# Block sums on Pool with their splits one step later, and the order of ACT's copies in the pair steps

## The chip, the cores and the metric

The kernel runs on one core of a Trainium2 chip. The metric is the device time of one execution in microseconds; the kernel before takes 726.09 us, the median of three runs (724.1 to 730.0).

## The reference

Three layers follow each other. Linear attention without softmax, with an RMS norm per head; a mixture of eight experts with one expert per token; and a two-layer network with an ELU, of width 2048. What comes out of the last is the result.

```python
kv = einsum('bhsd,bhse->bhde', k, v); out = einsum('bhsd,bhde->bhse', q, kv)
x = out / sqrt(mean(out * out) + 1e-6) * g_norm            # 2304 tokens x 512
e = argmax(x @ w_gate); p = softmax(x @ w_gate)[e]
y = p * (relu(x @ w1[e]) @ w2[e])                           # 8 experts, width 1024
h = y @ w_in; g = where(h > 0, h, exp(min(h, 0)) - 1)       # width 2048
return g @ w_out
```

## The kernel before, in words

Every product is made in full precision out of three fast ones: a value is split into a high word (a copy on ACT, `split_hi`, L521) and a low word (value minus high word, `split_lo`, L524, on DVE or Pool), and `three` multiplies high by high, low by high and high by low into one PSUM bank.

**Expert steps.** After the attention, the tokens lie sorted by expert. There are 64 steps `u` (8 experts by 8 pieces of their width), 37 and later in the part that matters here. `step(u)` issues the loads of unit u + 3 (`expert_load`, two DMAs on SP, into the six buffers of the tag "a", which prepared weights `f` share), the first product of unit u (`expert_h`: 12 matmuls into `ph`, then ACT's `hh` and DVE's `hl`), the second product of unit u − 1 (`expert_y`: 12 matmuls into four banks `acc`), and the split of unit u + 2's weights (`expert_split`: `w1h` and `w2h` on ACT, `w1l` and `w2l` on DVE). Some steps also split the next expert's tokens (`window`), or do a stage of preparing the weights of the third layer (`next(parts)`).

**Block sums.** The third layer multiplies `y` (in `yT`) by a Strassen-like scheme for most of its width: seven products of sums of blocks instead of eight. The seven right sides are y blocks and sums of y blocks; they are made once, split, and kept in `y_dram`. `y_block_into` splits a block of 384 tokens (ACT and Pool, four pieces) and stores it. `right_sums` makes the sums: a subtraction on DVE (L895), the split into `th` on ACT and `tl` on DVE, and two DMAs on SP (L885). One call of `next` finishes the sum before (low word and DMAs) and makes one sum with its high word. `early_sums` are 16 such sums, called at the end of the steps in `SUMS` (37, 38, 40, 44, 45, 46, 48, 52, 53, 54, 56, 60 to 64), the last one in the first steps of the next stage; `th` and `tl` have one buffer each (tag "e" has two). `late_sums` are eight, called in steps 1 to 9 of the next stage, with buffers in the unused half of `part`.

**Second block, first quarter.** 24 `ffn_step`s (six blocks by four pieces): first product `ffn_h` (12 matmuls), ACT's two exponential passes, DVE's `g`, then one step later its split (`ffn_g`), and two steps later the second product (`ffn_out`, 9 matmuls), whose accumulators ACT copies to `part` after the fourth piece. In the second step of a block `y_block_into` splits the next one.

**Pair steps.** The other three quarters of the width: `pair_step(w, s)`, 9 times two steps, each with seven products of six matmuls (`product`, L1064) named P1, P5, P2, P6, P3, P7, P4. P1, P6, P7 and P4 add up in one bank `pa`, and between them ACT copies the bank's present sum (`s1`, `u2`, `u3`); PE must wait for that copy before it adds the next product. DVE adds the other banks to the copies; that gives the four results g11, g12, g22 and the one from P4 (here g21). Each goes through `elu` (two ACT passes and one on DVE) and `elu_split`. In `gap(0)` to `gap(3)` stand second-layer products of earlier steps (`unit`, six matmuls and a DVE addition to `part`), and stages of preparing later weights (`next(parts2)`, with splits `ab` of weight sums).

**What sets the order.** All of this up to pair step w = 5 is under `manual_schedule`: each engine runs its instructions in the order in which the code issues them. The pair steps from w = 6 on and the last units are ordered by the framework's planner. Each engine is in order, and so is each queue: on SP a DMA that waits holds back all behind it.

Of the kernel before, what the change touches and what calls it, by code (L numbers as in the profile page):

```python
# [9 lines left out]
F32 = mybir.dt.float32  # L10
F32R = mybir.dt.float32r
# [4 lines left out]
ALU = mybir.AluOpType  # L16
# [25 lines left out]
def block_kernel(ctx, tc, qT, k, v, g_norm, w_gate, w1, w2, w_in, w_out, out, cap, **_):  # L42
# [477 lines left out]
    def split_hi(dst, src):  # L520
        return nc.scalar.activation(dst[0], src, AF.Copy)  # L521

    def split_lo(dst, src, engine):
        return engine.tensor_tensor(out=dst[1], in0=src, in1=dst[0].bitcast(F32), op=ALU.subtract)  # L524
# [50 lines left out]
    def expert_load(u):  # L575
        if u >= NU:
            return
        r, fc = divmod(u, NF)
        if fc == 0:
            load_regs(r)  # L580
        a1 = wst.tile([P, C], F32, name="a1", tag="a", bufs=AB)
        a2 = wst.tile([P, C], F32, name="a2", tag="a", bufs=AB)
        first = nc.sync.dma_start(out=a1, in_=w1[bass.ds(eids[r], 1), fc].rearrange("o p c -> (o p) c"))
        mark["sp"] = nc.sync.dma_start(out=a2, in_=w2[bass.ds(eids[r], 1), fc].rearrange("o p c -> (o p) c"))
        wstage[u] = (a1, a2)
        return first
# [286 lines left out]
            for h, t in enumerate((yh, yl)):  # L873
                nc.sync.dma_start(out=y_dram[n // 2, o][:, h], in_=t[:, k:k + KH].bitcast(F32))

    def right_sums(pieces, tiles):


        last = []

        def finish():
            m, o, k, r, t = last.pop()
            split_lo(t, r, nc.vector)
            for h in range(2):
                nc.sync.dma_start(out=y_dram[m, o][:, h, k], in_=t[h].bitcast(F32))  # L885

        for m, k in pieces:
            b = [[yT[:, h * KH + k, (2 * m + n) * BT:(2 * m + n + 1) * BT] for n in range(2)] for h in range(2)]
            r = None
            for o, x, y in ((5, b[1][1], b[0][1]), (3, b[0][1], b[0][0]), (4, b[1][1], None), (6, b[1][0], None)):  # L890
                if last:
                    finish()
                y = r if y is None else y
                r, t = tiles()
                nc.vector.tensor_tensor(out=r, in0=x, in1=y, op=ALU.subtract)  # L895
                split_hi(t, r)
                last.append((m, o, k, r, t))
                yield
        finish()
        yield  # L900

    def small_tiles():
        t = [hp.tile([P, BT], F32R, name=n, tag="e", bufs=2) for n in ("th", "tl")]
        return hp.tile([P, BT], F32, name="tr", tag="g", bufs=2), t


    assert 3 * (N // E) >= 2 * BT and 6 * (N // E) >= 4 * BT
    early_sums = right_sums([(m, k) for m in range(2) for k in range(KH)], small_tiles)
    SUMS = [u for u in range(4 * NF + 5, NU) if u % NF in (0, 4, 5, 6)]
    SUMS = SUMS[:8] + [u for u in SUMS[8:] if u > 6 * NF] + [NU - 1, NU]  # L910

    APART = 4 * NF + 4
    FIRST = NF + 1
# [3 lines left out]
    def step(u):  # L917
        r, fc = divmod(u, NF)
        if u == 4:
            nc.gpsimd.memset(xT[:, :, N:NS], 0.0)  # L920
        more = r + 1 < E and placed["t"] < need[r + 1]
        expert_load(u + 3)
        if u == FIRST - 1:
            prep_load(2)
        if u < NU:
            expert_h(u)
        q = QUOTA[u] if u < NF else 2 if more else 0
        if q:
            place(min(need[r + 1], placed["t"] + 1), 0)
        if u:  # L930
            expert_y(u - 1)
        if q > 1:
            place(min(need[r + 1], placed["t"] + q - 1), 0)
        if fc == 5 and r + 1 < E:
            place(need[r + 1], 0)
        place_ahead(2)
        expert_split(u + 2, nc.gpsimd if u < NF else nc.vector)
        if fc in (5, 6) and r + 1 < E:
            m = NP // 2
            window(r + 1, (fc - 5) * m, (fc - 4) * m)  # L940
        if FIRST <= u < NU and fc in (1, 2, 3, 7) and done["n"] < 6 * NC2:
            next(parts)
            done["n"] += 1
        if u == APART:
            place(NT, 0)
            beyond_windows()
        if u in SUMS:
            next(early_sums, None)
        if u == NU - 2 and cap >= BT:
            y_block_into(0)  # L950

# [79 lines left out]


    spare = part[:, NT // 2:].rearrange("p i c -> p (i c)")
    turn = {"n": 0}

    def spare_tiles():
        n = turn["n"] = 1 - turn["n"]
        at = [spare[:, (3 * n + i) * BT:(3 * n + i + 1) * BT] for i in range(3)]
        return at[0], (at[1].bitcast(F32R), at[2].bitcast(F32R))

    late_sums = right_sums([(NB // 2 - 1, k) for k in range(KH)], spare_tiles)
    NM = NB // 2
    steps = [(n, c) for n in range(NB) for c in range(NC2)]

# [72 lines left out]
    QUOTAS = ((6, 4), (6, 4), (6, 6))  # L1117
    pend = {}

    def finish_last():  # L1120
        if pend:
            elu_split(*pend.pop("x"))

    def pair_step(w, s):
        between = {n: [] for n in range(3)}
        if s == 0 and w:
            v = w - 1
            between[0] = [lambda: unit(v, 1, 0, 0), lambda: unit(v, 1, 0, 1)]
            between[1] = [lambda: unit(v, 0, 0, 1), lambda: unit(v, 0, 1, 1)]
            between[2] = [lambda: unit(v, 0, 2, 1), lambda: unit(v, 1, 1, 0), lambda: unit(v, 1, 1, 1)]  # L1130
        elif s == 0:
            between[0] = [lambda: ffn_out(*steps[-2], tiles=(0, 1))]
            between[1] = [lambda: ffn_out(*steps[-2], tiles=(2,))]
            between[2] = [lambda: ffn_out(*steps[-1], tiles=(0,))]
        else:
            v = w - 1
            if w:
                between[0] = [lambda: unit(v, 1, 2, 0), lambda: unit(v, 1, 2, 1)]
            else:
                between[0] = [lambda: ffn_out(*steps[-1], tiles=(1, 2))]  # L1140
            between[1] = [lambda: unit(w, 0, 0, 0)]
            between[2] = [lambda: unit(w, 0, 1, 0)]
            if w < NW - 1:
                between[2].append(lambda: unit(w, 0, 2, 0))
        quota = QUOTAS[w % NM][s]

        def gap(n):
            for _ in range(quota * (n + 1) // 4 - quota * n // 4):
                next(parts2, None)
            for f in between.get(n, []):  # L1150
                f()

        A, V = nc.scalar, nc.vector
        pa = ps_h.tile([P, C], F32, name="pa", tag="ph")
        pd = ps_x.tile([P, C], F32, name="pd", tag="pt")
        product(w, s, "P1", pa, True)
        s1 = wt.tile([P, BT], F32, name="s1")
        A.activation(s1, pa[:, :BT], AF.Copy)
        product(w, s, "P5", pd, True)
        s5 = wt.tile([P, BT], F32, name="s5", bufs=1)  # L1160
        A.activation(s5, pd[:, :BT], AF.Copy)
        pe = ps_x.tile([P, C], F32, name="pe", tag="pt")
        product(w, s, "P2", pe, True)
        finish_last()
        V.tensor_tensor(out=s1, in0=s1, in1=pe[:, :BT], op=ALU.add)
        g11 = elu(s1)
        gap(0)
        product(w, s, "P6", pa, False)
        u2 = hp.tile([P, BT], F32, name="u", tag="g", bufs=2)
        A.activation(u2, pa[:, :BT], AF.Copy)  # L1170
        elu_split(w, s, 0, 0, g11)
        product(w, s, "P3", pd, False)
        V.tensor_tensor(out=u2, in0=u2, in1=pd[:, :BT], op=ALU.add)
        g12 = elu(u2)
        gap(1)
        product(w, s, "P7", pa, False)
        u3 = hp.tile([P, BT], F32, name="u", tag="g", bufs=2)
        A.activation(u3, pa[:, :BT], AF.Copy)  # L1178
        elu_split(w, s, 1, 0, g12)
        V.tensor_tensor(out=s5, in0=s5, in1=u3, op=ALU.add)  # L1180
        g22 = elu(s5)
        gap(2)
        product(w, s, "P4", pa, False)
        elu_split(w, s, 1, 1, g22)
        pend["x"] = (w, s, 0, 1, elu(pa[:, :BT]))
        gap(3)

    def ffn_step(s):
        if 1 <= s <= len(steps):
            ffn_g(*steps[s - 1])  # L1190
        if s < len(steps):
            n, c = steps[s]
            ffn_h(n, c)
            if c == 1 and n + 1 < NB:
                y_block_into(n + 1)
        if 2 <= s < len(steps):
            ffn_out(*steps[s - 2])
        if s:
            next(early_sums, None)
            next(late_sums, None)  # L1200
            next(parts2)
        if s >= len(steps) - 4:
            for o in ((0, 3), (1, 4), (2, 5), (6,))[s - len(steps) + 4]:
                right_load(0, o)
# [9 lines left out]
    for w in range(by_hand, NW):  # L1214
        for s in range(2):
            pair_step(w, s)
    finish_last()

    w = NW - 1
    for b, t, ss in ((0, 2, (0,)), (1, 0, (0, 1)), (0, 0, (1,)), (0, 1, (1,)), (0, 2, (1,)), (1, 1, (0, 1)), (1, 2, (0, 1))):  # L1220
# [33 lines left out]
```

## Time and profile before

| | |
|---|---|
| median of three runs | 726.09 us |
| profiled execution | 724.72 us, span 722.9 us |
| PE busy, PEld busy | 683.1 us (94%), 628.6 us (87%) |
| DVE, ACT, POOL busy | 497.6 us (69%), 390.1 us (54%), 105.0 us (15%) |
| mean granted TensorE clock | 0.99 |
| data moved by DMA | 145.89 MB, mean 202 GB/s |

PE is the matmul, PEld the load of its weights, which runs beside the matmul before. Consecutive matmuls overlap in the records, so a busy PE need not be at its best; a PEld that is busy throughout is. The profile names an idle time by what released it ("<-"). Times of instructions contain the start and the end, which overlap with the neighbours: two DVE operations of 0.55 us can follow each other in 0.47 us.

### The profile page before, as it was taken

The page shows a single profiled execution, that of the slowest core. Times are in us where ns is not written, and L with a number is a line of the kernel's source. Part 1 is how long each engine was busy: PE and PEld are TensorE (multiplying, and loading weights), DVE is VectorE, ACT ScalarE, POOL GpSimd, SP SyncE. Part 2 cuts the span into 40 slices and gives each one's busy share as a digit, 9 for nine tenths or more (in the row PEclk, how much of TensorE's full clock was granted, in tenths as well). Part 3 has the DMA queues.
Part 4 walks back from the last instruction along what each step waited for, and adds up shares of the span by engine and source line. Part 5 has one row for each costly group of instructions (what it writes and reads, how often), then busy time and mean ns, then how long its engine had stood idle before and what let it go on. Part 6 is the DMA issues. An engine that isn't in the chain of part 4 may idle for free.

```text
span 722.9 us, 11978 instructions
## 1 busy us (share of the span) xinstructions
PE 683.1 (94%) x4236; PEld 628.6 (87%) x4236; DVE 497.6 (69%) x952; ACT 390.1 (54%) x818; POOL 105.0 (15%) x116
## 2 busy tenths in 40 slices
PE   8988999999989898969999998999999999999996
PEld 7888899999989887958789887988789898998895
DVE  4488768677776687747776646777687778955542
ACT  1463565555554564635665656664666555754550
POOL 7123851000000000022222200000000000002113
PEclk9998999999999999999999999999999999999999
DMA  8996956654555666744543627393637548165512
GB/s 281 395 310 166 295 175 197 185 176 147 187 164 177 216 199 220 218 175 149 197 173 116 260 119 290 134 342 120 264 113 311 230 163 321 59 261 219 205 57 88
DMA packets 67108, 145.89 MB, mean 202 GB/s; under 512 B 9312, under 2 KB 29280, under 8 KB 67040
## 3 DMA queue, kind: packets, MB, share of 16 engines
q1 hardware_dynamic: 63424, 135.44, 54.3%
q0 software_dynamic: 2880, 9.59, 3.8%
q8 instruction: 36, 0.59, 0.3%
q14 instruction: 32, 0.26, 0.1%
q10 hardware_dynamic: 736, 0.02, 0.1%
HBM read 118.92 MB, written 26.10 MB: 201 GB/s over the span
## 4 chain that ended last, share of the span: by engine, by line
PE 32%; issue 12%; DVE 10%; ACT 7%; DMA 3%; POOL 3%; SPq 0%; POOLq 0%; ACTq 0%; DVEq 0%
PE pa L1064 5%; PE acc L1105 3%; PE acc L1106 3%; PE acc L1104 3%; DMA y_dram<-th 3%; PE pd L1064 3%; PE ph L638 2%; PE ph L640 2%; POOL out L1112 2%; PE ph L639 2%; PE acc L1024 2%; PE acc L1025 2%; PE acc L1026 2%; PE pe L1064 1%; ACT e L1081 1%
## 5 line engine op out<-in xcount | busy, mean ns | idle before, releaser
L1064 PE MATMUL pa<-right,ab 128*128 128x384 f32 x432 | 86.1, 339 | 3.5 <-ACT u L1178 1.7
L1064 PEld LDWEIGHTS pa<-right,ab 128*128 128x128 f32 x432 | 76.7, 188 | 10.6 <-ACT u L1178 3.0
L638 PE MATMUL acc<-hh,w2h 128*128 128x288 f32 (+6 forms) x256 | 78.4, 306 | 7.7 <-ACT hh L657 7.7
L638 PE MATMUL ph<-xh,w1h 128*128 128x288 f32 (+6 forms) x256 | 78.2, 305 | 3.4 <-PEq L829 2.4
L640 PE MATMUL acc<-hl,w2h 128*128 128x288 f32 (+6 forms) x256 | 78.0, 305 | 0.0
L640 PE MATMUL ph<-xl,w1h 128*128 128x288 f32 (+6 forms) x256 | 77.7, 303 | 0.3 <-DVE xl L619 0.3
L639 PE MATMUL ph<-xh,w1l 128*128 128x288 f32 (+6 forms) x256 | 77.5, 303 | 0.0
L639 PE MATMUL acc<-hh,w2l 128*128 128x288 f32 (+6 forms) x256 | 77.0, 301 | 0.0
L1106 PE MATMUL acc<-w2h,gx 128*128 128x512 f32 x180 | 70.9, 394 | 0.0
L1105 PE MATMUL acc<-w2l,gx 128*128 128x512 f32 x180 | 70.7, 393 | 0.0
L1104 PE MATMUL acc<-w2h,gx 128*128 128x512 f32 x180 | 70.0, 389 | 0.0
L524 POOL TENSOR_TENSOR yl<-yT,yh 128x384 fp32r<-128x384 f32 x24 | 29.3, 1255 | 260.0 <-ACT yh L521 260.0
L658 DVE SCALAR_TENSOR_TENSOR hl<-ph,hh 128x288 fp32r<-128x288 f32 (+6 forms) x64 | 30.1, 470 | 49.8 <-ACT hh L657 49.7
L1112 POOL DMA_INDIRECT out<-part,ids x18 | 18.5, 1026 | 296.6 <-DVE part L1109 296.6
L657 ACT ACTIVATE hh<-ph 128x288 fp32r<-128x288 f32 (+6 forms) x64 | 26.7, 418 | 55.9 <-PE ph L640 55.5
L638 PEld LDWEIGHTS acc<-hh,w2h 128*128 128x128 f32 x256 | 48.5, 189 | 9.5 <-ACT hh L657 9.5
L524 DVE TENSOR_TENSOR w2l<-a,w2h 128x512 fp32r<-128x512 f32 x64 | 50.5, 789 | 7.9 <-ACT w2h L521 7.9
L638 PEld LDWEIGHTS ph<-xh,w1h 128*128 128x128 f32 x256 | 48.6, 190 | 3.8 <-ACTq L829 2.6
L640 PEld LDWEIGHTS acc<-hl,w2h 128*128 128x128 f32 x256 | 48.3, 188 | 1.6 <-DVE hl L658 1.5
L640 PEld LDWEIGHTS ph<-xl,w1h 128*128 128x128 f32 x256 | 48.6, 190 | 0.6 <-DVE xl L619 0.6
L639 PEld LDWEIGHTS ph<-xh,w1l 128*128 128x128 f32 x256 | 48.6, 190 | 0.0
L639 PEld LDWEIGHTS acc<-hh,w2l 128*128 128x128 f32 x256 | 48.4, 189 | 0.0
(219 smaller groups left out, 1647.8 us busy)
## 6 DMA issues: line engine op xcount, KB each, us to landing
right<-y_dram SPq DMA_DIRECT2D x63, 768.0 KB, 6.4
a<-w SPq DMA_DIRECT2D x128, 256.0 KB, 3.3
w<-w_in SPq DMA_DIRECT2D x16, 512.0 KB, 4.3
w<-w_out SPq DMA_DIRECT2D x16, 512.0 KB, 5.8
kt<-k SPq DMA_DIRECT2D x18, 256.0 KB, 6.6
vt<-v SPq DMA_DIRECT2D x18, 256.0 KB, 6.1
x_dram<-oz_all SPq DMA_DIRECT2D x18, 256.0 KB, 5.5
y_dram<-yh SPq DMA_DIRECT2D x9, 384.0 KB, 2.3
```

The costliest lines, as they stand in the source:

```text
L524: return engine.tensor_tensor(out=dst[1], in0=src, in1=dst[0].bitcast(F32), op=ALU.subtract)
L638: nc.tensor.matmul(out, lhsT=ah, rhs=bh, start=start, stop=False)
L639: nc.tensor.matmul(out, lhsT=al, rhs=bh, start=False, stop=False)
L640: nc.tensor.matmul(out, lhsT=ah, rhs=bl, start=False, stop=stop)
L657: nc.scalar.activation(hh[:, :W], ph[:, :W], AF.Relu)
L658: nc.vector.scalar_tensor_tensor(out=hl[:, :W], in0=ph[:, :W], scalar=0.0, in1=hh[:, :W].bitcast(F32), op0=ALU.max, op1=ALU.subtract)
L1024: nc.tensor.matmul(acc, lhsT=gh[:, ts], rhs=w2h, start=(c == 0), stop=False)
L1064: nc.tensor.matmul(ps[:, :BT], lhsT=x[:, cs], rhs=b[:, y, k], start=(start and k == 0 and n == 0), stop=(k == KH - 1 and n == 2), skip_gro ...
L1104: nc.tensor.matmul(acc, lhsT=gh[:, ts], rhs=w2h, start=(s == 0 and c == 0), stop=False)
L1105: nc.tensor.matmul(acc, lhsT=gh[:, ts], rhs=w2l, start=False, stop=False)
L1106: nc.tensor.matmul(acc, lhsT=gl[:, ts], rhs=w2h, start=False, stop=(s == 1 and c == 1))
L1112: put = nc.gpsimd.indirect_dma_start(out=out, out_offset=bass.IndirectOffsetOnAxis(ap=ids[:, i:i + 1], axis=0), in_=part[:, i], in_offset= ...
```

## The change

Four things. In `right_sums` the subtraction and the low word move from DVE to Pool, and one call of `next` now makes the high word, the low word and the DMAs of the sum before, and only the subtraction of its own. The early sums are called at the head of a step, ahead of `expert_load`, in another list of 17 steps that ends at 60; nothing of them is left for the next stage. In the pair steps ACT's copies of `pa` and `pd` stand ahead of the exponentials of results that are ready earlier, and the exponentials of the P4 bank and the splits of g22 and g21 move into the next step (behind the last pair step they stand by themselves). `s1` gets one buffer instead of two, `s5` two instead of one.

```diff
-    def right_sums(pieces, tiles):
+    def right_sums(pieces, raw_tile, split_tiles):
         def finish():
-            m, o, k, r, t = last.pop()
-            split_lo(t, r, nc.vector)
+            m, o, k, r = last.pop()
+            t = split_tiles()
+            split_hi(t, r)
+            split_lo(t, r, nc.gpsimd)
             for h in range(2):
                 nc.sync.dma_start(out=y_dram[m, o][:, h, k], in_=t[h].bitcast(F32))
...
-                r, t = tiles()
-                nc.vector.tensor_tensor(out=r, in0=x, in1=y, op=ALU.subtract)
-                split_hi(t, r)
-                last.append((m, o, k, r, t))
+                r = raw_tile()
+                nc.gpsimd.tensor_tensor(out=r, in0=x, in1=y, op=ALU.subtract)
+                last.append((m, o, k, r))
...
-    SUMS = [u for u in range(4 * NF + 5, NU) if u % NF in (0, 4, 5, 6)]
-    SUMS = SUMS[:8] + [u for u in SUMS[8:] if u > 6 * NF] + [NU - 1, NU]
+    SUMS = (37, 38, 40, 41, 43, 44, 45, 46, 49, 51, 52, 53, 54, 56, 57, 58, 60)
...
         more = r + 1 < E and placed["t"] < need[r + 1]
+        if u in SUMS:
+            next(early_sums)
         expert_load(u + 3)
...
-        if u in SUMS:
-            next(early_sums, None)
...
-        s1 = wt.tile([P, BT], F32, name="s1")
+        s1 = wt.tile([P, BT], F32, name="s1", bufs=1)
         A.activation(s1, pa[:, :BT], AF.Copy)
+        if pend:
+            g21 = elu(pend["c21"])
         product(w, s, "P5", pd, True)
-        s5 = wt.tile([P, BT], F32, name="s5", bufs=1)
+        s5 = wt.tile([P, BT], F32, name="s5")
         A.activation(s5, pd[:, :BT], AF.Copy)
+        if pend:
+            elu_split(*pend["g22"])
         pe = ps_x.tile([P, C], F32, name="pe", tag="pt")
         product(w, s, "P2", pe, True)
-        finish_last()
+        if pend:
+            elu_split(*pend["at"], g21)
         V.tensor_tensor(out=s1, in0=s1, in1=pe[:, :BT], op=ALU.add)
-        g11 = elu(s1)
         gap(0)
         product(w, s, "P6", pa, False)
         u2 = hp.tile([P, BT], F32, name="u", tag="g", bufs=2)
         A.activation(u2, pa[:, :BT], AF.Copy)
-        elu_split(w, s, 0, 0, g11)
+        g11 = elu(s1)
         product(w, s, "P3", pd, False)
         V.tensor_tensor(out=u2, in0=u2, in1=pd[:, :BT], op=ALU.add)
-        g12 = elu(u2)
         gap(1)
         product(w, s, "P7", pa, False)
         u3 = hp.tile([P, BT], F32, name="u", tag="g", bufs=2)
         A.activation(u3, pa[:, :BT], AF.Copy)
-        elu_split(w, s, 1, 0, g12)
         V.tensor_tensor(out=s5, in0=s5, in1=u3, op=ALU.add)
-        g22 = elu(s5)
+        elu_split(w, s, 0, 0, g11)
+        g12 = elu(u2)
         gap(2)
         product(w, s, "P4", pa, False)
-        elu_split(w, s, 1, 1, g22)
-        pend["x"] = (w, s, 0, 1, elu(pa[:, :BT]))
+        elu_split(w, s, 1, 0, g12)
+        g22 = elu(s5)
+        pend.update(c21=pa[:, :BT], g22=(w, s, 1, 1, g22), at=(w, s, 0, 1))
         gap(3)
...
-            next(early_sums, None)
             next(late_sums, None)
...
-    finish_last()
+    elu_split(*pend["g22"])
+    elu_split(*pend["at"], elu(pend["c21"]))
```

The tiles of the late sums are cut anew out of the same spare space: two for subtractions and two pairs for splits, where there were two sets of three.

## Rows read from the trace of the kernel before

**Rows 1.** The table of stretches: the stretch (us from the span's start) and its length; busy time of PE, PEld, DVE, ACT and POOL, with the number of instructions; granted clock of TensorE; mean share of the DMA engines; GB/s.

```profile
120.00:210.00 90.00, 90.00 (x626) 90.00 (x625) 67.68 (x119) 49.41 (x100) 0.00 (x0) 1.00 0.56 175
...
219.40:312.28 92.88, 85.15 (x638) 81.75 (x636) 70.20 (x133) 51.24 (x108) 0.00 (x0) 0.99 0.63 201
312.28:320.83 8.55, 6.72 (x38) 5.44 (x36) 3.06 (x5) 2.42 (x7) 4.55 (x4) 1.00 0.65 253
320.83:330.00 9.17, 4.55 (x16) 4.25 (x16) 5.02 (x7) 5.58 (x13) 2.46 (x3) 0.81 0.16 63
330.00:370.00 40.00, 36.52 (x177) 31.27 (x177) 30.15 (x50) 24.70 (x54) 10.81 (x10) 1.00 0.52 183
370.00:424.08 54.08, 54.08 (x273) 48.98 (x272) 34.12 (x60) 32.72 (x71) 11.53 (x9) 1.00 0.52 200
424.08:450.60 26.52, 24.26 (x122) 21.17 (x121) 15.84 (x36) 16.59 (x38) 0.00 (x0) 1.00 0.49 180
450.60:547.95 97.35, 95.26 (x470) 84.41 (x469) 73.54 (x151) 56.88 (x125) 0.00 (x0) 1.00 0.56 210
547.95:711.00 163.05, 163.02 (x810) 146.12 (x809) 109.94 (x214) 90.83 (x192) 14.64 (x14) 1.00 0.50 189
```

**Rows 2.** The chain of waits in order of time: start, length, what. Twelve matmuls into `pa` are P4 of one pair step and P1 of the next; between these two rows lie two pair steps.

```profile
546.90 2.10 PE pa L1064 x12
...
578.15 2.10 PE pa L1064 x12
```

**Rows 3.** The list of waits of the whole span: engine, what waited and for what; us in total, times, longest.

```profile
ACT th L521 <- DMA y_dram<-th: 24.9, 8, 6.1
...
PE acc L638 <- ACT hh L657: 7.7, 8, 2.6
...
PE ph L638 <- DVE g L1005: 5.8, 2, 4.6
...
PE acc L1024 <- ACT part L1029: 2.2, 2, 1.3
PE pa L1064 <- ACT u L1178: 1.7, 3, 0.7
...
PE pa L1064 <- ACT u L1170: 1.5, 2, 1.1
...
PE ph L640 <- POOL yl L524: 1.1, 3, 0.5
```

**Rows 4.** The timeline of ACT in steps with early sums: start, length, engine, line, operation; in brackets the idle time before it and what ended that.

```profile
237.70 0.52 ACT L521 ACTIVATE th<-tr 128x384 fp32r<-128x384 f32 x1 [5.41 <-DMA y_dram<-th]
...
254.32 0.53 ACT L521 ACTIVATE th<-tr 128x384 fp32r<-128x384 f32 x1 [1.99 <-DMA y_dram<-th]
254.75 0.39 ACT L657 ACTIVATE hh<-ph 128x288 fp32r<-128x288 f32 x1
...
258.64 0.52 ACT L521 ACTIVATE th<-tr 128x384 fp32r<-128x384 f32 x1 [1.91 <-DVE tr L895]
259.07 0.39 ACT L657 ACTIVATE hh<-ph 128x288 fp32r<-128x288 f32 x1
```

**Rows 5.** The timeline of SP's queue in the same stage: the moment of the issue and its length.

```profile
230.23 0.37 SPq L885 DMA_DIRECT2D y_dram<-th  x1
234.18 0.33 SPq L885 DMA_DIRECT2D y_dram<-tl  x1
234.76 0.34 SPq L583 DMA_DIRECT2D a<-w  x1
```

**Rows 6.** The timelines of ACT and PE at the start of the second block.

```profile
320.73 0.53 ACT L521 ACTIVATE th<-tr 128x384 fp32r<-128x384 f32 x1 [6.13 <-DMA y_dram<-th]
...
325.61 0.44 PE L638 MATMUL ph<-yh,w1h 128*128 128x384 f32 x1 [4.62 <-DVE g L1005]
```

**Rows 7.** The timelines of DVE and POOL: two DVE operations of a sum with Pool idle; four low words of a y block on Pool (348.18 to 353.18), and two DVE operations beside them; another four on Pool (from 313.17) and DVE's `hl` beside them.

```profile
304.95 0.55 DVE L524 TENSOR_TENSOR tl<-tr,th 128x384 fp32r<-128x384 f32 x1
305.42 0.55 DVE L895 TENSOR_TENSOR tr<-yT,tr 128x384 f32<-128x384 f32 x1
...
348.18 5.00 POOL L524 TENSOR_TENSOR yl<-yT,yh 128x384 fp32r<-128x384 f32 x4 [15.91 <-ACT yh L521]
...
349.52 1.36 DVE L895 TENSOR_TENSOR part<-yT 128x384 f32<-128x384 f32 x1
350.80 1.51 DVE L716 TENSOR_TENSOR cvt_a<-cvt_a,cvt_b 128x512 int32<-128x512 int32 x1
...
313.17 4.55 POOL L524 TENSOR_TENSOR yl<-yT,yh 128x384 fp32r<-128x384 f32 x4 [198.75 <-ACT yh L521]
...
314.63 0.42 DVE L658 SCALAR_TENSOR_TENSOR hl<-ph,hh 128x256 fp32r<-128x256 f32 x1 [2.56 <-ACT hh L657]
```

**Rows 8.** Pool's low words of all y blocks (ns, shortest, median and longest), and DVE's low words of the weights between 219.4 and 312.28 us, with Pool idle (busy us, mean ns).

```profile
L524 POOL TENSOR_TENSOR yl<-yT,yh x24: 1000/1326/1502, 313.2 to 402.4; 128x384 fp32r<-128x384 f32 x24
...
L524 DVE TENSOR_TENSOR w1l<-a,w1h 128x512 fp32r<-128x512 f32 x25 | 17.2, 690 | 2.4 <-ACT w1h L521 1.4
```

**Rows 9.** The experts' weight loads (tile `a`, 256 KB each): us from issue to landing.

```profile
DMA to landing us min/median/max: 2.6/3.3/7.9
```

More of the change, by code (lines that the diff above doesn't have):

```diff
@@ L900, in right_sums, with raw_small, split_small @@
         yield
-    def small_tiles():
-        t = [hp.tile([P, BT], F32R, name=n, tag="e", bufs=2) for n in ("th", "tl")]
-        return hp.tile([P, BT], F32, name="tr", tag="g", bufs=2), t
+    def raw_small():
+        return hp.tile([P, BT], F32, name="tr", tag="g", bufs=2)
+    def split_small():
+        return [hp.tile([P, BT], F32R, name=n, tag="e", bufs=2) for n in ("th", "tl")]
     assert 3 * (N // E) >= 2 * BT and 6 * (N // E) >= 4 * BT
-    early_sums = right_sums([(m, k) for m in range(2) for k in range(KH)], small_tiles)
-    SUMS = [u for u in range(4 * NF + 5, NU) if u % NF in (0, 4, 5, 6)]
-    SUMS = SUMS[:8] + [u for u in SUMS[8:] if u > 6 * NF] + [NU - 1, NU]
+    early_sums = right_sums([(m, k) for m in range(2) for k in range(KH)], raw_small, split_small)
+    SUMS = (37, 38, 40, 41, 43, 44, 45, 46, 49, 51, 52, 53, 54, 56, 57, 58, 60)
+    assert SUMS[0] > 3 * NF and SUMS[8] > 6 * NF
     APART = 4 * NF + 4
@@ L1033, in block_kernel, with spare_part, raw_spare, split_spare @@
     spare = part[:, NT // 2:].rearrange("p i c -> p (i c)")
[L1034 to L1041, printed above, removed]
+    turn = {"r": 0, "s": 0}
+    def spare_part(n):
+        return spare[:, n * BT:(n + 1) * BT]
+    def raw_spare():
+        turn["r"] += 1
+        return spare_part(turn["r"] % 2)
+    def split_spare():
+        turn["s"] += 1
+        return [spare_part(2 + 2 * (turn["s"] % 2) + h).bitcast(F32R) for h in range(2)]
+    late_sums = right_sums([(NB // 2 - 1, k) for k in range(KH)], raw_spare, split_spare)
     NM = NB // 2
@@ L1118, in block_kernel @@
     pend = {}
-    def finish_last():
-        if pend:
-            elu_split(*pend.pop("x"))
     def pair_step(w, s):
```

## The prediction, made before the result was known

> **What bounds the kernel now.** I read the stage table first [rows 1]. Its columns of interest are PE and PEld. From 120 to 210 us (expert steps, no block sums) PE and PEld are busy for all 90 us, with DVE at 67.7 and ACT at 49.4: TensorE alone sets the pace there. From 547.95 on PE is busy for 163.02 of 163.05 us. Whatever can be won lies between 219 and 548 us, so I worked out what each stretch there loses against a TensorE that never waits:
>
> - Expert steps 37 to 63 (219.4 to 312.28): PEld is busy 81.75 of 92.88 us, and 90 of 90 where nothing is late. Lost: **11.1 us**.
> - Change to the second block (312.28 to 330): the first piece of 8.55 us has PEld 5.44 and PE 6.72, so 1.8 to 3.1 are lost, I take 2.5. The second piece runs 16 matmuls in 9.17 us; 370 to 424 runs 273 in 54.08, 0.198 us each, so 16 are worth 3.2 us and 6.0 are lost, part of it at a lower granted clock (0.81). Lost: **8.5 us**.
> - Steps 330 to 370: 177 matmuls at 0.198 are 35.1 of 40 us. Lost: **4.9 us**. From 370 on, PE is busy throughout.
> - Pair steps: 424.08 to 450.60 has 26.52 − 24.26 = 2.3 us of idle PE. 450.60 to 547.95 takes 97.35 us for three groups of two steps; the chain of waits shows one group to take 578.15 − 546.90 = 31.25 us where PE never waits [rows 2], so 97.35 − 93.75 = 3.6 are lost. Together **5.9 us**.
>
> That is 30.4 us. The list of waits says who is late [rows 3]: PE waits for ACT's `hh` (7.7 us, 8 times), for DVE's `g` (5.8, twice), for ACT's copies `part` (2.2) and `u` (1.7 and 1.5), for Pool's `yl` (1.1). Behind `hh` and `g` stands ACT waiting for the copy `th` of an earlier sum to leave by DMA: 24.9 us, 8 times.
>
> The timelines show how. In a step with a sum ACT does `th` last, and that waits for DVE's subtraction at the end of DVE's queue and for the buffer of the sum before. At 237.70 ACT had stood still for 5.41 us because of that DMA; in a quiet run of sums, `hh` follows `hh` after 259.07 − 254.75 = 4.3 us [rows 4], while a step of 24 matmuls needs 24 × 81.75 / 636 = 3.1 us of PEld [rows 1]. SP shows the same loop: the DMA of `th` goes out at 230.23, that of `tl` at 234.18, and only then the next weights at 234.76 [rows 5]. At 320.73 ACT had waited 6.13 us for the last sums' DMAs, and PE then stood 4.62 us until 325.61 [rows 6].
>
> **The change, part by part.**
>
> *Early sums.* Each of the 16 moves a subtraction and a low word from DVE to Pool. The split into high and low word comes one sum later, at the head of the step. ACT's `th` then needs an `r` that was made a whole step or more ago, and a buffer whose DMA was sent at the head of the previous sum. ACT has a hole there: it has finished the weights' high words and waits for PE's next `ph`. I cost `th` at nothing, hidden under that wait; uncovered, it costs its 0.5 us [rows 4] per sum, 8 us in all.
>
> Pool's cost: DVE takes one such operation every 305.42 − 304.95 = 0.47 us; Pool took 5.00 us for four of the same size [rows 7], 1.25 each, with DVE at work beside it. Two per step are 2.5 us of a 3.1 us step: Pool, idle here today, carries it. What it does to DVE is the unknown. Beside Pool, DVE's subtraction took 1.36 us instead of 0.55 and the 512-wide one 1.51 instead of 0.69 [rows 7, 8], about 0.8 us per Pool operation, more than the 0.47 that it saves. But `hl`, which reads one operand from PSUM, took its usual 0.42 while Pool ran. Bounds per Pool operation: 0 to 0.85 us of DVE. I take half: the Pool work stands at the head of a step, where DVE is between two steps' work, so that DVE comes out about as loaded as before (32 × 0.42 = 13.4 us against 32 × 0.47 = 15). DVE is then no bound: 70.2 busy of what would be 82 us.
>
> SP: both DMAs now stand ahead of the step's two weight loads, and `tl` waits for Pool. The loads go out about 2.3 us into the step (`th` 0.5 after the old ACT work, Pool 0.85 to 1.25, issue 0.3) and are needed some 3 us later; they land after 2.6 to 7.9 us, median 3.3 [rows 9]. So up to 1 us lateness per step, mostly inside the slack of a split that runs a step ahead of its matmuls. Before, loads stood behind `tl` in the same way. I leave 2.5 us of stalls here, from this and from DVE: **−8.6** (bounds: −11.1, and +23 in the second rival).
>
> *Sums done by step 60, not 65.* The first y block's splits (steps 62 and after) no longer share ACT with `th`, nor its exponentials. The 6.13 us wait and the 4.62 us of PE behind it go [rows 6], with the clock's dip. Next in line are Pool's four `yl`, which start as soon as ACT is free; I leave 0.5: **−8.0** (bounds −8.5, −6).
>
> *Late sums.* Eight sums in the first nine steps of the second block, the same move. ACT no longer waits for DVE's end of step, but its split now waits for a Pool queue that also holds four `yl` of 1.0 to 1.5 us [rows 8] in every fourth step: about 4 × 1.3 + 2 × 1.3 = 7.8 us, started 3.4 us into a step of 21 × 0.198 = 4.2, so ACT may stand some 3 us. PE needs those steps' `gh` and `g` only 4 us later, so I cost that at nothing in PE; without that slack it is 3 us, twice. I leave 1.3: **−3.6** (bounds −4.9, +1).
>
> *Pair steps.* No operation is added. The copies out of `pa` go ahead of exponentials, so that PE's 3.2 us of waits for `u` [rows 3] and the restarts behind them should go; what remains are waits for the `ab` splits. The exponentials of the P4 block and the split of g22 move into the next step. Unit (1,0), second half, needs g22 about 5 us into that step; ACT's copy, relu, exp, copy, split and DVE's low word reach it after about 4.4 (first copy at 1.5 us, then six operations near 0.5). I cost it at nothing; uncovered it is some 0.5 us in each of 17 steps, 8 us. I leave 1.5: **−4.4** (bounds −5.9, +4). Behind the last step the same chain has no products to hide under: **+1** (0 to 2). The two buffer counts exchanged keep as many bytes: nothing.
>
> Sum: −8.6 −8.0 −3.6 −4.4 +1.0 = −23.6. The profiled execution took 724.72 us (span 722.9 and 1.8 around it), 1.4 below the median of the runs, 726.09. 724.7 − 23.6 = 701.1, and as a median near 702.5; I say **702 us**.
>
> **The rivals.**
>
> *Pool and DVE stand in each other's way.* Every Pool operation costs DVE the full 0.85 us. In the expert steps 32 × 0.85 = 27 us replace 15, so DVE needs 70.2 − 15 + 27 = 82.2 us in a stretch where PE needs 82: both are the bound. If 30% of DVE's present 22.7 us of idle stay as waits, the stretch takes 89 us, and 3.8 of the 8.6 are left; in the late sums the gain is nil. 702 + 4.8 + 3.6 = **710 us**. For: the 1.36 and 1.51 us rows [rows 7]. Against: `hl` is untouched, and a third of DVE's time is free where PE is bound [rows 1]. A rule of the Trainium skill speaks for this rival and against the change: SBUF — State Buffer, "Who interferes with whom", says that a VectorE instruction with two SBUF inputs and a GpSimd instruction that reads SBUF exclude each other, the second waiting for the first to finish. By that rule the time is this rival's; the trace agrees for single operations (1.36 us beside Pool) and can't show how often they meet.
>
> *Weights starve behind Pool on SP (slower).* If loads under this order land late, each sum's step is set by a loop over two steps: `th` 0.45, Pool 1.3, two issues 0.7, landing L, two high words 1.3, so (3.75 + L)/2 per step. At L = 3.3 it is 3.5 us; at 6.5 it is 5.1, 2 us over PE's 3.1, 34 us over 17 steps in place of 11.1. 702 + 34 − 2.5 is no less than **733 us**. It turns from gain to loss near L = 5.5: 17 × 1.5 = 26 us lost here where I left 2.5, which eats the whole 23.6. For: landings up to 7.9 us [rows 9]. Against: 201 GB/s in this stretch [rows 1], and the median.
>
> *The pair steps gain nothing*, because the waits there come from prepared weights that ACT does anyway, and the last third, which a planner orders, changes for the worse: 702 + 5 = **707 us**.
>
> **How the numbers follow.** Forecast 0.58 (its own range 695 to 708), pair steps nothing 0.12, Pool against DVE 0.20, starving weights 0.07; 0.03 below 693, where nearly all of the 30.4 us would be won. Of the Pool rival's 0.20, 0.12 lie near 710 and 0.08 above 716, where weights come late as well. So the range 693 to 716 leaves out 0.07 + 0.08 + 0.03 = 0.18. About 1% is what a measurement can tell here (724.1 to 730.0 over three runs). Faster by more: 0.58 + 0.12 + 0.03 + 0.12 = 0.85; within 1%: 0.08; slower: 0.07.
>
> **What would show it.** Right: no wait of ACT for DMA from `y_dram`; PEld near 100% between 219 and 300 us; PE without a gap over 1 us near 320; no PE wait for `u`. Pool rival: DVE's `w1l`, `w2l` means well over 0.69 us and PE waiting for `hl` or `gl`. Starving: ACT's `w1h` waiting for weights by far more than today. What would make me wrong most easily is ACT standing behind Pool's `yl` in the second block.

## The result, and the profile after

The changed kernel takes **709.09 us** (median of 4 runs, 706.70 to 709.89) against 726.40 us for the kernel before on the same chip (4 runs, 724.10 to 730.00): a ratio of 0.975 (0.971 to 0.980). The prediction was 702 us, within 693 to 716. The profiled execution took 708.56 us; the one before took 724.72, so 16.2 us are gone where the sum said 23.6.

The span and the first part of the page:

```profile
span 706.8 us, 11988 instructions
...
PE 677.4 (96%) x4236; PEld 628.6 (89%) x4236; DVE 493.3 (70%) x904; ACT 388.6 (55%) x818; POOL 160.4 (23%) x164
```

PEld is where it was (628.6 us), Pool has 55 us more. To see where the time went I cut both executions at the same pieces of work, not at the same times: ACT's first `hh`, its `hh` of step 37 and of step 63, and the first and last copy `s` out of `pa` in the pair steps. ACT's timeline before:

```profile
79.82 0.46 ACT L657 ACTIVATE hh<-ph 128x352 fp32r<-128x352 f32 x1 [1.14 <-PE ph L640]
...
219.80 0.41 ACT L657 ACTIVATE hh<-ph 128x288 fp32r<-128x288 f32 x1 [5.55 <-PE ph L640]
...
314.24 0.36 ACT L657 ACTIVATE hh<-ph 128x256 fp32r<-128x256 f32 x1
...
425.34 0.49 ACT L1158 ACTIVATE s<-pa 128x384 f32<-128x384 f32 x1 [0.95 <-PE pa L1064]
...
691.49 0.49 ACT L1158 ACTIVATE s<-pa 128x384 f32<-128x384 f32 x1
```

and after:

```profile
83.26 0.46 ACT L657 ACTIVATE hh<-ph 128x352 fp32r<-128x352 f32 x1 [2.31 <-PE ph L640]
...
223.58 0.41 ACT L657 ACTIVATE hh<-ph 128x288 fp32r<-128x288 f32 x1 [5.40 <-PE ph L640]
...
315.22 0.37 ACT L657 ACTIVATE hh<-ph 128x256 fp32r<-128x256 f32 x1
...
416.29 0.49 ACT L1163 ACTIVATE s<-pa 128x384 f32<-128x384 f32 x1 [0.95 <-PE pa L1073]
...
675.32 0.49 ACT L1163 ACTIVATE s<-pa 128x384 f32<-128x384 f32 x1
```

| stretch | before | after | difference | predicted |
|---|---|---|---|---|
| start to first `hh` | 79.82 | 83.26 | +3.4 | 0 |
| first `hh` to step 37 | 139.98 | 140.32 | +0.3 | 0 |
| **A**: step 37 to step 63 | 94.44 | 91.64 | −2.8 | −8.6 |
| **B**: step 63 to first `s` | 111.10 | 101.07 | −10.0 | −8.0 − 3.6 |
| **C**: first `s` to the end of the span | 297.56 | 290.51 | −7.05 | −4.4 + 1.0 |

The pieces have the letters A, B and C from here on. So at least two thirds of the expected gain in the expert steps are missing, and the pair steps gave twice what I gave them. The same cuts as a table by stage (columns as in [rows 1]):

```profile
223.58:315.22 91.64, 83.32 (x627) 80.34 (x627) 69.22 (x106) 54.76 (x115) 37.42 (x33) 1.00 0.66 221
315.22:332.00 16.78, 16.78 (x98) 15.72 (x98) 9.74 (x14) 8.96 (x21) 10.53 (x10) 1.00 0.46 175
332.00:372.00 40.00, 39.89 (x198) 35.28 (x197) 31.16 (x42) 27.10 (x58) 25.60 (x22) 1.00 0.53 190
...
416.29:442.90 26.61, 26.61 (x139) 24.28 (x138) 18.72 (x42) 20.56 (x47) 0.00 (x0) 1.00 0.56 214
442.90:534.30 91.40, 91.40 (x458) 82.52 (x457) 72.64 (x148) 53.31 (x119) 0.00 (x0) 1.00 0.58 223
```

In the rows from 315.22 on PE hardly stands still, and the dip of the granted clock to 0.81 [rows 1] is gone: almost no wait of PE is left in B and in the pair steps. (Behind the last `s` it is busy for 25.41 of 31.48 us, before as after.) The expert steps still have holes: PE 83.32 of 91.64. The list of waits of the whole span says what became of [rows 3]:

```profile
POOL tl L524 <- ACT th L521: 43.5, 11, 7.6
...
ACT w1h L521 <- DMA a<-w: 22.8, 16, 2.9
...
PE ph L638 <- issue: 4.4, 1, 4.4
...
ACT th L521 <- DMA y_dram<-th: 4.2, 2, 3.7
...
PE acc L640 <- DVE hl L658: 4.1, 4, 1.5
...
PE acc L638 <- ACT hh L657: 1.3, 1, 1.3
```

ACT's 24.9 us behind `y_dram` have shrunk to 4.2, PE's 7.7 behind `hh` to 1.3, and no wait of PE for `g` or `u` is in the list. But ACT now waits 22.8 us, 16 times, for the **weights** `a`. In the list of the kernel before that wait stood at 4.1 us:

```profile
ACT w1h L521 <- DMA a<-w: 4.1, 6, 1.4
```

How that comes about is in two timelines of the kernel after, SP's:

```profile
237.31 0.33 SPq L887 DMA_DIRECT2D y_dram<-th  x1
238.59 0.33 SPq L887 DMA_DIRECT2D y_dram<-tl  x1
239.17 1.03 SPq L583 DMA_DIRECT2D a<-w  x1
240.46 0.34 SPq L584 DMA_DIRECT2D a<-w  x1
```

and ACT's:

```profile
236.25 0.62 ACT L521 ACTIVATE w2h<-a 128x512 fp32r<-128x512 f32 x1
236.77 0.51 ACT L521 ACTIVATE th<-tr 128x384 fp32r<-128x384 f32 x1
...
242.55 0.63 ACT L521 ACTIVATE w1h<-a 128x512 fp32r<-128x512 f32 x1 [2.32 <-DMA a<-w]
```

ACT makes `th` only when the weights' high words are done (236.77), SP sends it at 237.31, waits for Pool's `tl` until 238.59, and only then sends the next weights, whose high word starts at 242.55 after 2.32 us of waiting. Late weights make `th` late, and a late `th` the next weights; e4 below tests this.

### The profile page after: what moved, and what is told of

It reads as the page before. It is cut to its first block, busy times and chain, and to the rows that moved or that the text cites. A ratio compares the mean times of both kernels' runs of the same rounds, so it can differ in the third digit from the quotient of the medians.

```text
span 706.8 us, 11988 instructions
## 1 busy us (share of the span) xinstructions
PE 677.4 (96%) x4236; PEld 628.6 (89%) x4236; DVE 493.3 (70%) x904; ACT 388.6 (55%) x818; POOL 160.4 (23%) x164
## 4 chain that ended last, share of the span: by engine, by line
PE 48%; issue 6%; DMA 6%; POOL 4%; DVE 3%; ACT 2%; POOLq 0%; SPq 0%; ACTq 0%; DVEq 0%
PE pa L1073 10%; PE acc L1114 6%; PE acc L1115 6%; PE acc L1113 6%; PE pd L1073 5%; DMA a<-w 3%; PE pe L1073 3%; PE acc L1029 2%; PE acc L1028 2%; PE acc L1027 2%; PE ph L638 2%; PE ph L640 2%; PE ph L639 2%; POOL tl L524 1%; DMA y_dram<-tl 1%
## 5 line engine op out<-in xcount | busy, mean ns | idle before, releaser
L524 DVE TENSOR_TENSOR w2l<-a,w2h 128x512 fp32r<-128x512 f32 x64 | 54.7, 855 | 9.4 <-ACT w2h L521 8.7
L521 ACT ACTIVATE w1h<-a 128x512 fp32r<-128x512 f32 x64 | 40.1, 627 | 22.9 <-DMA a<-w 22.8
L524 DVE TENSOR_TENSOR w1l<-a,w1h 128x512 fp32r<-128x512 f32 x56 | 42.4, 758 | 13.9 <-ACT w1h L521 12.3
```

## The experiments

All runs are compared with the kernel before, run beside them on the same chip; stretches come from one profile of each. Up to step 63 the changed kernel, e2 and e9 run the same code, and A reads 91.64, 93.70 and 93.39 us in them; the kernel before and e1 do so too, with 94.44 and 93.43. One reading of A is good to some 2 us. Part of that is the cut at step 37: from the first `hh` to step 63 the first three take 231.96, 232.22 and 232.23 us, the other two 234.42 and 231.85.

| run | median | ratio (95%) | A | B | C |
|---|---|---|---|---|---|
| changed kernel | 709.09 | 0.975 (0.971–0.980) | 91.64 | 101.07 | 290.51 |
| e1, pair steps alone | 719.17 | 0.991 (0.988–0.994) | 93.43 | 111.09 | 290.47 |
| e2, sums alone | 715.89 | 0.985 (0.980–0.990) | 93.70 | 100.99 | 297.68 |
| e3, early sums on DVE | 706.08 | 0.970 (0.965–0.975) | 90.07 | 101.07 | 290.45 |
| e4, loads first | 702.23 | 0.966 (0.962–0.971) | 85.09 | 101.17 | 290.47 |
| e6, loads first, DVE | 698.96 | 0.962 (0.959–0.965) | 83.26 | 101.18 | 290.53 |
| e7, loads first, spread | 697.23 | 0.959 (0.955–0.962) | 79.90 | 101.17 | 290.48 |
| e8, sums to step 64 | 707.48 | 0.974 (0.971–0.977) | 86.44 | 105.35 | 290.52 |
| e9, late sums at once | 711.54 | 0.980 (0.977–0.983) | 93.39 | 103.05 | 290.48 |
| **e10, loads first, spread, DVE** | **692.41** | 0.956 (0.954–0.959) | 80.26 | 101.12 | 290.50 |
| e11, old form, new places | 724.99 | 1.000 (0.999–1.002) | 103.23 | 103.17 | 297.71 |
| e12, old form, spread, new pair steps | 709.50 | 0.979 (0.976–0.981) | 93.04 | 103.06 | 290.52 |
| e13, as e10, sum at the end of the step | 700.56 | 0.968 (0.965–0.972) | 85.84 | 100.88 | 290.42 |

**1. The two halves, each alone.** e1 is the kernel before with the new pair steps; e2 is the changed kernel with the pair steps of before.

```diff
 # e1, against before (e2 undoes the same against after)
         A.activation(s1, pa[:, :BT], AF.Copy)
+        if pend:
+            g21 = elu(pend["c21"])
...
-        finish_last()
+        if pend:
+            elu_split(*pend["at"], g21)
...
-        g11 = elu(s1)
...
-        elu_split(w, s, 0, 0, g11)
+        g11 = elu(s1)
```

> The kernel before with only the new order of the pair steps and the tail; sums as before. By the prediction's term (-4.4 + 1) about 3 us under the kernel before, 0.995 of it. If the pair steps' gain read from the trace of the changed kernel (7 us between the first copy of a pair step and the end) is theirs alone, 0.990. By the rival that they gain nothing: 1.00.

> The changed kernel with the pair steps as before. If the parts add up: slower than the changed kernel by what e1 gains, so 712 to 716 us, 0.98 to 0.985 of the kernel before. If the pair steps gain nothing: 709. The stretch from hh of step 37 to hh of step 63 stays near 91.6 us as in the changed kernel.

Measured: C falls by 7.1 us in e1 and stays in e2; B does the reverse (10.1 us less in e2), and A moves in neither by more than a reading's scatter. 0.991 × 0.985 = 0.976: the halves add up. The pair steps are worth some 7 us, not 3.4.

**2. What holds the expert steps: Pool or the weights?** e3 puts both operations of the early sums back on DVE; e4 only changes two lines' order.

```diff
 # e3, in right_sums, for the early sums
-            split_lo(t, r, nc.gpsimd)
+            split_lo(t, r, nc.vector)
...
-                nc.gpsimd.tensor_tensor(out=r, in0=x, in1=y, op=ALU.subtract)
+                nc.vector.tensor_tensor(out=r, in0=x, in1=y, op=ALU.subtract)
 # e4, in step
-        if u in SUMS:
-            next(early_sums)
         expert_load(u + 3)
+        if u in SUMS:
+            next(early_sums)
```

> The changed kernel with both operations of the early sums back on DVE, everything else (place, order, split one sum later) as in the changed kernel. Theory 'port' (Pool and DVE in each other's way cost most of what was not won in the expert steps): the stretch of steps 37 to 63 falls from 91.6 to 86 us or less, total 704. Theory 'weights' (loads late behind the sums' DMAs on SP): the low word comes 0.6 us sooner to SP, so 1 to 2 us better at most, unless DVE's full queue delays the low word, then worse by 3. Theory 'buffer' (high word waits for the DMA of the sum before): no change, 709.

> The changed kernel with the step's two weight loads issued ahead of the sum's DMAs on SP; ACT, DVE and Pool in the same order. Theory 'weights': ACT's waits of w1h for weights fall from 22.8 us to under 8, the stretch of steps 37 to 63 from 91.6 to 87 us, total 704 to 705. Theory 'buffer': the sums' DMAs land behind half a megabyte of weights, ACT's th waits rise from 4.2 us to 10 or more, total 709 to 714. Theory 'port': no change.

Measured: e3 gains 1.6 us in A, within what a reading scatters and far from the 86 us of theory 'port', and the weights stay late (19.7 us, 15 times). e4 gains 6.55 us in A with the same instructions, as theory 'weights' said (6.5 counted from the first `hh`). Its waits:

```profile
ACT th L521 <- DMA y_dram<-th: 13.8, 6, 4.1
...
ACT w1h L521 <- DMA a<-w: 4.3, 4, 2.3
...
PE acc L640 <- DVE hl L658: 0.4, 2, 0.2
```

ACT's wait for weights goes from 22.8 to 4.3 us, and PE's for `hl` with it. What takes its place is `th` behind the DMA of an earlier `th`, the wait that the change had almost removed: it had only been covered by the lateness of the weights. Theory 'buffer' was right that this wait would come, and wrong that it would eat the gain.

**3. What is left after that, and what the prediction's terms were worth.** e6 is e4 with e3's edit. e7 is e4 with the sums spread; e8 is the changed kernel with them close to their old places; e9 has the eight late sums in the old form.

```diff
 # e7, against e4
-    SUMS = (37, 38, 40, 41, 43, 44, 45, 46, 49, 51, 52, 53, 54, 56, 57, 58, 60)
+    SUMS = (25, 28, 31, 34, 38, 41, 44, 47, 49, 51, 53, 54, 56, 57, 59, 60, 62)
 # e8, against after
+    SUMS = (37, 38, 40, 44, 45, 46, 48, 52, 53, 54, 56, 58, 60, 61, 62, 63, 64)
 # e9, against after; right_sums_at_once and spare_tiles are those of before
-    late_sums = right_sums([(NB // 2 - 1, k) for k in range(KH)], raw_spare, split_spare)
+    late_sums = right_sums_at_once([(NB // 2 - 1, k) for k in range(KH)], spare_tiles)
```

> The changed kernel with the next weights sent ahead of the sum's DMAs and, besides, both operations of the 16 early sums (subtraction and low word) on DVE in place of Pool. Loads first with Pool took 85.09 us for expert steps 37 to 63, against some 82 without any lateness, and 702.2 us in all. Theory buffer (what is left is ACT's th waiting for the DMA of an earlier th): nothing in it depends on the engine, so 85 us again, th waiting 10 to 15 us for y_dram, 702 us. Theory port (what is left is Pool holding DVE up): w1l and w2l back near 0.69 and 0.79 us, 83 us for the stretch, 700 us. Third possibility, DVE as a second bound with 32 operations more of 0.47 us (15 us on top of 73 busy of 85, less what Pool no longer slows): 87 us, 704 us.

> The changed kernel with the next weights sent ahead of the sum's DMAs, and the 17 steps with a sum spread over steps 25 to 62 in place of 37 to 60, mostly two or three steps apart. Loads first took 225.5 us from the first hh to that of step 63, and 702.2 us. Theory buffer (th waits 13.8 us, 6 times, for the DMA of an earlier th, because sums stand in neighbouring steps): those waits fall under 4 us, and the way from the first hh to step 63 takes 222.5 to 224 us, 700 us in all. Theory port (each Pool operation costs DVE something wherever it stands): as many operations, so 225.5 and 702 us. Against both: the last sums end at step 62 again, and the splits of the first y block stand behind their DMAs, which would cost up to 3 us in the change to the second block (101.1 us from step 63 to the first s1 before).

> The changed kernel with nothing altered but the steps of the early sums: close to the old places (37, 38, 40, 44, 45, 46, 48, 52, 53, 54, 56, 58, 60, 61, 62, 63, 64), so that the last ones again stand beside the splits of the first y block. The way from hh of step 63 to the first copy of the pair steps took 111.1 us before the change and takes 101.1 with it. If the early end of the sums is worth the 8 us that the prediction put on it, this way takes 107 to 109 us and the kernel some 715 us. If the gain comes from the new form of the sums (Pool, the split a step later) and not from their places, it takes 101 to 103 us and the kernel 709 us or less, since weights are late in fewer steps before step 60.

> The changed kernel with the eight late sums in the old form (subtraction, high word and low word of one sum together, on DVE), everything else as changed. If the new form of the late sums is worth the 3.6 us that the prediction put on it, the way from hh of step 63 to the first copy of the pair steps goes from 101.1 to about 104.7 us, and the kernel to 712.7 us, with ACT waiting for DVE's subtraction in that stretch. If the whole 10 us come from the end of the early sums, it stays at 101 to 102 us and the kernel at 709 us. Up to 1 us faster if Pool's yl were held up by the late sums.

Measured, one by one. **e6**: A 83.26, 1.8 less than e4, as the port theory said; but `th` still waits 11.3 us, so neither theory is all of it. **e7**: A falls to 79.90 us, and the table by stage shows the floor of this stretch:

```profile
223.35:303.25 79.90, 79.83 (x626) 79.31 (x626) 68.56 (x106) 53.16 (x111) 32.66 (x27) 1.00 0.73 240
303.25:404.42 101.17, 101.03 (x518) 91.22 (x517) 66.77 (x100) 62.92 (x135) 46.34 (x39) 1.00 0.52 191
```

PE is busy for 79.83 of 79.90 us; `th` waits 5.1 us in place of 13.8, and the way to step 37 got no longer by the sums that moved there (140.6 us from the first `hh`; 140.3 in e4). The last sum at step 62 costs B nothing. **e8**: the end at step 60 is worth 4.3 us of B, between the two theories, but A is 5.2 us shorter without it, and the ratio is the same (0.974 and 0.975): between these two lists the places only decide in which stretch a sum's cost is paid. The second theory has the total and named the reason, weights late in fewer steps, without its size. **e9**: the late sums' new form is worth 2.0 us of B, not 3.6.

**4. Places, form, and the best of both.** e10 is e7 with e3's edit. e11 is the kernel before with the new list `SUMS` and nothing else; e12 is e1 with the list of e7. e13 is e10 with the sum issued where the kernel before had it.

```diff
 # e11, against before
-    SUMS = [u for u in range(4 * NF + 5, NU) if u % NF in (0, 4, 5, 6)]
-    SUMS = SUMS[:8] + [u for u in SUMS[8:] if u > 6 * NF] + [NU - 1, NU]
+    SUMS = (37, 38, 40, 41, 43, 44, 45, 46, 49, 51, 52, 53, 54, 56, 57, 58, 60)
 # e13, against e10
         expert_load(u + 3)
-        if u in SUMS:
-            next(early_sums)
...
+        if u in SUMS:
+            next(early_sums)
         if u == NU - 2 and cap >= BT:
```

> The changed kernel with loads first, the sums spread over steps 25 to 62, and both operations of the early sums on DVE: the two better variants together. Spread alone took 697.2 us; its steps 37 to 63 took 79.90 us with PE busy for 79.83, so TensorE was the only bound there. Theory that Pool beside DVE matters only where DVE is a bound: nothing left to win, 79.8 to 80.5 us for the stretch and 697 us in all. Theory that DVE on this work is cheaper wherever it stands (it won 2 to 3 us with the sums close together): 1 to 2 us less, 695 to 696 us. If 32 operations more on DVE make it the bound in steps 25 to 36: up to 3 us more.

> The kernel before with nothing altered but the list of steps that carry the early sums: the places of the change (37 to 60) with the old form (subtraction, high and low word of one sum at the end of the step, on DVE, loads ahead). It tells places from form. If ending at step 60 is worth the 8 us by itself, the way from hh of step 63 to the first copy of the pair steps goes from 111.1 to 103 us, and the kernel to about 718 us if steps 37 to 63 stay as long; those may grow, since 17 sums then stand in 24 steps: up to 4 us. If the old form is what costs (as the run with the late sums as of old and the new places of the early ones suggests: 103.1), expect the same 103. If the form decides and the places don't, 109 to 111.

> The kernel before with the new pair steps and the early sums spread over steps 25 to 62, all sums in the old form on DVE. Theory that density is what costs in the expert steps: ACT's th waits for y_dram all but vanish (from 24.9 us to under 6), steps 37 to 63 take 80 to 82 us, the second block 103 to 104 us (late sums in the old form 2 us above the new), so about 700 to 702 us, and the new form of the early sums gains next to nothing over good places. Theory that the form is needed (ACT's th behind DVE's subtraction at the end of each step): 85 to 88 us for the stretch, 705 us or more.

> The best variant so far (loads first, sums spread over steps 25 to 62, early sums on DVE; 692.4 us, steps 37 to 63 in 80.26 us) with each sum issued at the end of its step, where the kernel before had it, in place of behind the loads at its head. The split still comes one sum later. It tells the two halves of the new form apart: the delay of the split, and the place at the head of the step. If the delay is what counts (ACT's th finds its input ready and its buffer long free), 80 to 82 us and 692 to 694 us. If the place counts (at the head ACT would otherwise only wait for ph, at the end th stands between the weights' high words and the next hh, and its buffer is asked for as late), 85 to 93 us, PE waiting for hh, and 697 to 705 us.

Measured. **e11**: no change at all (1.000). The table by stage shows why:

```profile
219.59:322.82 103.23, 89.05 (x626) 84.07 (x626) 72.88 (x138) 53.93 (x114) 1.99 (x3) 0.95 0.62 198
322.82:425.99 103.17, 101.28 (x518) 91.16 (x517) 67.55 (x116) 62.77 (x136) 27.12 (x23) 1.00 0.50 186
```

B falls by 7.9 us, almost exactly the 8.0 of the prediction, and A grows by 8.8: together 206.4 us where the kernel before took 205.5. PE's waits for `hh` went from 7.7 to 13.7 us, and the dip of the granted clock moved as well: 0.95 in A (0.99 in [rows 1]), 1.00 in B. **e12**: spreading doesn't shorten A in the old form, 93.04 against 93.43 in e1, and in that stretch

```profile
ACT th L521 <- DMA y_dram<-th: 19.3, 6, 4.2
ACT th L521 <- DVE tr L895: 13.8, 6, 3.3
```

so my theory of density falls for A. Yet e12 is clearly under e1 (0.979 against 0.991): B is 8.0 us shorter, and the way from the first `hh` to step 63 only 4.2 us longer (236.06 and 231.85). Sums that are spread, and not only moved, bring something in the old form too. **e13** keeps the delayed split and gives up the place: A 85.84. Up to step 63 it differs from e12 in the delay alone, and that is worth 7.2 us of A. `th` waits only 1.5 us for `y_dram`, but `w1h` 22.2 us for weights (1.5 in e10), since the sum's DMAs stand right ahead of the next step's loads again:

```profile
ACT w1h L521 <- DMA a<-w: 22.2, 16, 2.3
```

The time is that of e13's second theory, the mechanism is not: no wait of PE for `hh` is in its list.

**e10** has the delay and the place, and is the fastest: 692.41 us, 2% under the changed kernel (0.956 against 0.975, intervals far apart). Its table by stage:

```profile
218.22:298.48 80.26, 79.17 (x626) 79.14 (x625) 68.87 (x131) 53.29 (x112) 2.00 (x3) 1.00 0.73 243
298.48:399.60 101.12, 100.99 (x518) 91.20 (x517) 67.45 (x100) 62.87 (x136) 45.52 (x38) 1.00 0.50 190
```

With TensorE busy for 79.17 of 80.26 us, DVE instead of Pool can win nothing in A (80.26 against 79.90), as the first theory said. Its runs are 4.8 us under e7's all the same, but they were taken beside runs of the kernel before that took 2.7 us less; as ratios the two overlap. In the profiles 3.4 of the 4.8 us lie ahead of the first `hh` (79.4 and 82.7 us), in code that neither changes.

## Why the prediction was right and wrong

The total fell inside the stated range, but outside the forecast's own 695 to 708. It stands beside the 710 of the Pool rival, whose mechanism it is not. The sum was off in both directions: too hopeful by 5.8 us in A, 3.4 at the start and 1.6 in the late sums, too cautious by 3.65 in the pair steps and the tail. That these left no more than 7.5 us is luck. Of the signs named for the forecast, the gap near 320 and the waits for `u` are gone; PEld, which was to be near 100% in the expert steps, is busy for 80.34 of A's 91.64 us.

The losses themselves were read well. For the expert steps and the second block the prediction has 11.1 + 8.5 + 4.9 = 24.5 us, and in e7, where PE hardly waits, A and B take 24.5 us less than before (205.54 and 181.07; 23.5 less than in e1). What failed is how much of them the change was said to leave. Worked through in its own order:

**Early sums, −8.6: wrong, −2.8.** Over all profiles with the same code (three and two) A fell by only 1.0 us, so even the 2.8 is no firm gain. The floor of A is 79.9 us (e7), so the kernel before lost 14.5 us there (I read 11.1) and the changed one still loses 11.7. The step that failed is "I leave 2.5 us of stalls here", and in it "Before, loads stood behind `tl` in the same way". They did, but the trace before could not show what that costs, because ACT was late for another reason; e13, with that order and the other reason gone, takes 5.6 us more than e10, and waits for weights. Taken one after the other, loads ahead of the sum's DMAs win 6.55 us (e4), DVE in place of Pool 1.8 (e6), spreading 3.0 (e10): 11.4 of the 11.7. In another order the shares differ: spreading wins 5.2 ahead of DVE (e7), and DVE then nothing (e10). The share of the loads is shown by e4, and e13 agrees; DVE's is the size of a reading's scatter, though e3 has it too.

I had the figure in hand. My own loop for the starving rival, (3.75 + L)/2, gives 3.5 us per step at the usual landing of 3.3 us, against the 3.1 that TensorE needs: 0.4 × 17 = 7 us, close to the 6.55 of e4; an estimate, since no run timed the loop by itself. I worked it out only for late landings and charged nothing for the usual one. The rival was right as a mechanism, and its sign came: ACT's `w1h` waits 22.8 us for weights, 4.1 before. Only its turning point to a slower kernel was not reached.

**Sums done by step 60, −8.0: right in its stretch, worth nothing by itself.** PE's 4.62 us gap and the clock's dip are gone, and e11 measures 7.9 us in B (e8, in the new form, 4.3). But e11 and e8 show that the same sums then cost as much in A: 206.4 against 205.5 us for A and B with the old form, and 192.7 against 191.8 (e8) with the new one. I took the moved sums to be free in A, so this term hung on the first one. For A and B together the prediction had −20.2; measured −12.8, and e8, close to the old places, has −13.75: what was won came from the form. It is not that one loss was counted twice: in e10, where a sum costs next to nothing, A and B together are 24.2 us shorter than before.

**Late sums, −3.6: −2.0** by e9, and by e11 and e12, which end at 103.1 too. ACT's wait behind Pool's queue, which I named as the likeliest way to be wrong, is in the trace (`part` for Pool's `part`, 9.3 us, 6 times; for DVE's it was 9.4 before) and costs PE nothing, as costed. PE is busy for 100.96 of B's 101.07 us, so the missing 1.6 us are no wait that is left: less was to be won here than I read.

**Pair steps, −4.4, and tail, +1.0: too small, −7.05 together.** For the first stretch I took the idle time of PE, 2.3 us. Counting matmuls says more: 0.191 us each (26.61 / 139) in the kernel after make the 122 of [rows 1] worth 23.4 us, so 3.2 were lost; for the 470 of the other stretch 0.200 each (91.40 / 458) confirm the 3.6. That is an estimate of 6.7 us in all. In the first stretch a matmul before took 0.199 us of busy time (24.26 / 122), so part of the loss lay inside the busy column. Nothing of the 1.5 us that I left stayed. The tail cost nothing: from the last `s` to the end every profile, with the old order or the new, takes 31.41 to 31.50 us.

**The start, +3.4, was not in the sum.** PE waits 4.4 us at the first matmul of the first expert step (`issue` in the list above), in code that the change does not touch. It is scatter: e1, with the code of before in that place, takes 82.09 us to the first `hh`.

**Pool against DVE.** The 710 us of this rival are nearly what was measured, for the wrong reason: e3 and e6 put Pool's share of A at 1.6 to 1.8 us, near the scatter, not at the 4.8 the rival gave the expert steps. Lines of DVE from 224 to 304 us, after:

```profile
L524 DVE TENSOR_TENSOR w1l<-a,w1h 128x512 fp32r<-128x512 f32 x22 | 18.7, 849 | 8.6 <-ACT w1h L521 8.3
```

and in e10:

```profile
L524 DVE TENSOR_TENSOR w1l<-a,w1h 128x512 fp32r<-128x512 f32 x24 | 16.5, 687 | 0.9
```

A low word takes 849 ns with Pool at work and 687 without. Added up over DVE's rows in A, the operations other than the sums' take some 12 us longer in the changed kernel than in e3, 0.4 us for each of the 31 operations that Pool has there: the 0.42 that the forecast took, and half of the rival's 0.85. Little of it reaches the time (e3 is 1.6 us shorter in A): DVE is busy for 69.22 of A's 91.64 us and has room for it. The Trainium skill (SBUF — State Buffer, "Who interferes with whom") has a VectorE instruction with two SBUF inputs and a GpSimd instruction that reads SBUF exclude each other. The two means agree with it in direction, and e10 against e7 shows that it costs nothing where TensorE is the bound.

## What to carry to other kernels

On an in-order queue, what waits for nothing goes ahead of what waits for another engine: moving the next loads ahead of two small writes won 6.55 us, and moving 32 operations to an idle engine won nothing that the runs show (e3, e6). Taking the input of a split from a step earlier did: with the sums spread, the delay is worth 7.2 us (e12, e13). When a wait is to be removed, work out the loop that remains at its usual durations, not only at bad ones, and look for the wait that the old one covered. And where each item brings its loss along, moving the items out of a stretch can cost elsewhere what it gains there (e11); both gains come in full only when the loss per item is gone (e10).

## What was not expected of the hardware

The way to the first `hh` took 79.38 to 84.25 us in profiles of kernels whose code up to there does the same. What decides it was not tried. Nor was a second pair of buffers for `th` and `tl`: how much of the 3.0 us of spreading is the wait for the buffer stays open.
